# Attention scores as single float32 products, with deeper buffers and a new order table

## The chip, the cores and the metric

The kernel runs on one core of one Trainium2 chip. The metric is device time in microseconds (us) of one execution; lower is better. The engines are TensorE (PE in the profile; PEld are its weight loads), VectorE (DVE), ScalarE (ACT), GpSimd (POOL) and SyncE (SP), which here only issues DMAs.

## What is computed

Local and global attention for 4 batches, 8 heads, 512 local and 32 global tokens and a head size of 64, and behind it two networks over the 2,176 tokens of width 512:

```python
s_g = scale * q_g @ k_all.T;  out_g = softmax(s_g) @ v_all        # global rows see all 544 keys
s_ll = where(|i - j| <= 32, scale * q_l @ k_l.T, -1e9)            # local rows: a band,
out_l = softmax([scale * q_l @ k_g.T, s_ll]) @ [v_g, v_l]         # and the 32 global keys
x = concat(out_g, out_l)                                           # to (2176, 512)
x = (sigmoid(x @ w_gate) * (x @ w_val)) @ w_out                    # 1536 inner columns
h = x @ w_in;  out = (P(h) / (Q(h) + 1e-6)) @ w2_out               # 2048 inner columns; P, Q polynomials
```

The change touches the attention alone.

## The kernel before

**Stages.** `attention` comes first, then `gated` and `rational` (the two networks). TensorE takes its instructions in program order, so the networks' first matmul (line 539) stands behind the attention's last.

**Units.** The attention works on 16 units, one for a batch and a pair of heads. The 512 queries of a unit are 4 blocks of 128, each against a window of 224 keys. `units[u]` with even `u` also does the global rows of the units `u` and `u+1` (all steps whose name begins with `g_`).

**Split products.** A product of float32 precision is made as three products of `F32R` parts: high by high, high by low, low by high (`three`, and the loop in `s_mm`). So `k_hi` and `q_hi` (ScalarE casts) and `k_lo` and `q_lo` (GpSimd differences) split what was loaded ahead of `s_mm`; `g_q` splits the global queries; `v_hi`, `v_lo`, `t_hi`, `t_lo` split the values and the transposed probabilities.

**Steps of a unit.** `s_mm` (scores of two blocks: a "half", each block as two heads on the two halves of the rows), `s_max` (adds the mask, takes the maxima, writes `p`), `s_exp`, `s_add` and `s_rec` (sums and reciprocals), `s_norm` (VectorE takes 3 of the half's 4 rows of `p`, GpSimd one), `t_mm` (transposes of `p` and of the global probabilities `pgn`), `t_hi`, `t_lo`, `v_mm` (times the values, 6 matmuls a block), `v_xs` and `v_xg` (local and global results out of PSUM), `x_out` (GpSimd splits both into `xh`, `xl`, the networks' input). `v_dma` moves the values of neighbour blocks.

**Order.** `STEPS` is a table of places in unit steps: step `name` of unit `u` stands at `u + place`, and all are written to the engines in the order of these places. `w_raw` to `w_lo` are the steps that fetch and split the networks' first four weights (`Weights`, unchanged), in the same table. Each engine takes its own instructions in this order.

**Places.** PSUM has four places of `[128, 2, 512]` (`pair`), handed round in the order in which steps ask for them: scores, global scores, transposes and results all take one, and a place comes free when VectorE or ScalarE has read it. In SBUF, most tiles have two buffers.

Of the kernel before, what the change touches and what calls it, by code (L numbers as in the profile page):

```python
# [35 lines left out]
def tile_of(tok):  # L36
# [13 lines left out]
    (-0.696, 'k_hi'),  # L50
    (-0.612, 'q_hi'),
    (-0.595, 'w_mag'),
    (-0.434, 'k_lo'),
    (-0.361, 'q_lo'),
    (-0.351, 'w_bits'),
    (-0.222, 'w_add'),
# [2 lines left out]
    (0.380, 's_max', 0),
    (0.465, 's_max', 1),  # L60
    (0.577, 's_exp', 0, (2, 3)),
    (0.725, 'load', 'v'),
    (0.746, 's_exp', 0, (0, 1)),
    (0.792, 's_add', 0),
    (0.836, 'g_mm'),
    (0.860, 's_exp', 1, (2, 3)),
    (0.878, 'g_max'),
    (0.912, 'v_hi'),
    (0.920, 's_rec', 0),
    (0.945, 'w_hi'),  # L70
    (0.962, 'v_lo'),
    (1.014, 'g_exp'),
    (1.053, 's_norm', 0, 0, 3),
    (1.061, 'g_add'),
    (1.165, 'g_rec'),
    (1.200, 's_exp', 1, (0, 1)),
    (1.224, 'w_lo'),
    (1.231, 'g_norm'),
    (1.276, 's_norm', 0, 3, 4),
    (1.333, 's_add', 1),  # L80
    (1.606, 't_mm', 0),
    (1.635, 's_rec', 1),
    (1.657, 't_hi', 0),
    (1.681, 't_lo', 0),
    (1.683, 't_mm', 1),
    (1.758, 's_norm', 1, 3, 4),
    (1.775, 'v_dma'),
    (1.845, 's_norm', 1, 0, 3),
    (1.859, 't_hi', 1),
    (1.862, 'v_mm', 0),  # L90
    (1.863, 't_mm', 2),
    (1.883, 't_lo', 1),
    (1.916, 'v_mm', 1),
    (1.990, 't_mm', 3),
    (2.026, 't_hi', 2),
    (2.032, 'v_xs', 0),
    (2.081, 'v_xg', 0),
    (2.113, 't_lo', 2),
    (2.117, 't_hi', 3),
    (2.199, 't_lo', 3),  # L100
    (2.593, 'v_mm', 2),
# [30 lines left out]

def attention(ctx, tc, ident, xh, xl, ins, other={}, others=0):
# [24 lines left out]

# [25 lines left out]
    def g_load(u, x):  # L184
        nc.sync.dma_start(dict(q=qgn, v=vgn)[x], ins[f"{x}_g"])

    def g_q(u):
# [1 line left out]
        t = st[u]["qg"] = [two.tile([128, 6 * SG], F32R, tag=f"qg{s}", name=f"qg{s}{u}") for s in "hl"]
        src = qgn[:, b, pr // 2]  # L190
        nc.scalar.mul(t[0], src, -0.125)
        nc.vector.scalar_tensor_tensor(t[1], src, -0.125, t[0].bitcast(F32), ALU.mult, ALU.subtract)
# [4 lines left out]

    def k_hi(u):
        k = st[u]["k"] = two.tile([128, 2, NBLK, WIN], F32R, tag="k", name=f"k{u}")
        nc.scalar.copy(k[:, 0], st[u]["kn"])  # L200

    def k_lo(u):
        k = st[u]["k"]
        nc.gpsimd.tensor_tensor(k[:, 1], st[u]["kn"], k[:, 0].bitcast(F32), ALU.subtract)

    def q_hi(u):
        s = st[u]
        s["qh"] = two.tile([128, NBLK, 128], F32R, tag="qh", name=f"qh{u}")
        nc.scalar.copy(s["qh"], s["qn"])

    def q_lo(u):
        s = st[u]
        s["ql"] = two.tile([128, NBLK, 128], F32R, tag="ql", name=f"ql{u}")
        nc.gpsimd.tensor_tensor(s["ql"], s["qn"], s["qh"].bitcast(F32), ALU.subtract)
# [152 lines left out]
    def v_xg(u, half):
        s = st[u]
        at = 0 if u % 2 else 256
        if half == 0:  # L370
# [4 lines left out]
        nc.vector.tensor_tensor(s["xg"], s["po"][:, 1, at : at + 64], s["xg"], ALU.add)

    def x_out(u):
        b, pr = units[u]
        xs, xg = st[u]["xs"].rearrange("p c t -> p (c t)"), st[u]["xg"]
        parts = [(slice(64 * j, 64 * j + 64), B * S + b * SG, xg[64 * j : 64 * j + 64, SG * j : SG * j + SG])  # L380
                 for j in range(2)]
        for t0, n in TILES:
            lo, hi = max(t0, b * S), min(t0 + n, (b + 1) * S)
            if lo < hi:
                parts.append((slice(0, 128), lo, xs[:, lo - b * S : hi - b * S]))
        for rows, tok, src in parts:
            i, off = tile_of(tok)
            n = src.shape[1]
            h, l = xh[i][rows, pr, off : off + n], xl[i][rows, pr, off : off + n]
            copy(h, src, rows)  # L390
            nc.gpsimd.tensor_tensor(l, src, h.bitcast(F32), ALU.subtract)
# [3 lines left out]
    steps = dict(g_q=g_q, load=load, k_hi=k_hi, k_lo=k_lo, q_hi=q_hi,  # L395
                 q_lo=q_lo, v_hi=v_hi, v_lo=v_lo, v_dma=v_dma, s_mm=s_mm, s_max=s_max, s_exp=s_exp, s_add=s_add,
                 s_rec=s_rec, s_norm=s_norm, g_mm=g_mm, g_max=g_max, g_exp=g_exp, g_add=g_add, g_rec=g_rec,
                 g_norm=g_norm, t_mm=t_mm, t_hi=t_hi, t_lo=t_lo, v_mm=v_mm, v_xs=v_xs, v_xg=v_xg, x_out=x_out)
# [1 line left out]
    for x in "qv":  # L400
        g_load(0, x)
    for u in range(2):
        load(u, "k")
        load(u, "q")
        other["w_raw"](u)
    for u in range(2):
        load(u, "v")
# [464 lines left out]
```

## Time and profile before

| | us |
|---|---|
| median of 3 runs (lowest, highest) | 1041.23 (1040.93, 1043.89) |
| the profiled execution | 1040.94 |
| its span in the trace | 1039.1 |
| attention, up to the networks' first matmul | 231.0 |
| networks, from there to the end of the span | 808.1 |

TensorE is busy for 94% of the span, VectorE 72%, ScalarE 62% and GpSimd 59%. These are means over two stages that differ, so the stages are to be read one by one.

### The profile page before, as it was taken

Reading aid. Unit: us, or ns where it says so; the run is one execution under the profiler, and the core shown is the slowest. Engines: PE = TensorE matmul, PEld = TensorE weight load, DVE = VectorE, ACT = ScalarE, POOL = GpSimd, SP = SyncE. Lnnn points to the kernel's source line nnn. Section 1 sums busy time; section 2 is a strip of 40 time slices with the busy share of each in tenths; the row PEclk is TensorE's granted clock in tenths of the full one; section 3 lists DMA queues with packets and bytes.
Section 4 is the critical chain, followed back from the end, with each engine's and each line's share of the span. In section 5 each row is a group of like instructions: output and inputs, shape, how many; then the busy total and the mean of one; then the engine's idle time right before and its main releaser. Section 6 shows DMA issues by size and latency. Waiting matters only on the chain.

```text
span 1039.1 us, 15083 instructions
## 1 busy us (share of the span) xinstructions
PE 975.2 (94%) x5184; PEld 866.9 (83%) x5184; DVE 745.9 (72%) x1364; ACT 646.2 (62%) x1312; POOL 611.5 (59%) x592
## 2 busy tenths in 40 slices
PE   4788878879999999999999999999999999999996
PEld 3667777768998988989989989889888988988895
DVE  5877777754766676666666743797778888888885
ACT  5788877754444444444444433887777777777783
POOL 6899999963444444443444443664457556665663
PEclk9999998999999999999999999999999999999999
DMA  7343334222443444344434441100220130010111
GB/s 258 102 110 110 110 110 109 74 72 61 144 158 125 129 156 133 130 151 133 142 122 152 139 156 58 65 1 7 87 70 1 41 122 1 1 61 22 41 71 62
DMA packets 55921, 98.65 MB, mean 95 GB/s; under 512 B 5284, under 2 KB 29988, under 8 KB 55844
## 3 DMA queue, kind: packets, MB, share of 16 engines
q1 hardware_dynamic: 55844, 97.69, 29.5%
q8 instruction: 41, 0.67, 0.3%
q14 instruction: 36, 0.29, 0.1%
HBM read 69.62 MB, written 21.23 MB: 87 GB/s over the span
## 4 chain that ended last, share of the span: by engine, by line
PE 73%; DVE 1%; POOL 1%; issue 1%; ACT 1%; POOLq 0%; DVEq 0%
PE rp L733 6%; PE rp L732 6%; PE rp L731 6%; PE rp L541 6%; PE rp L539 6%; PE rp L540 6%; PE pg L539 4%; PE pg L540 4%; PE pg L541 4%; PE pv L540 4%; PE pv L539 4%; PE pv L541 4%; PE p L584 4%; PE p L583 4%; PE p L582 4%
## 5 line engine op out<-in xcount | busy, mean ns | idle before, releaser
L663 POOL TENSOR_TENSOR v<-v,u 128x384 f32<-128x384 f32 (+1 forms) x80 | 96.3, 1204 | 112.7 <-ACT v L659 112.2
L706 POOL TENSOR_TENSOR rgl<-t,rgh 128x384 fp32r<-128x384 f32 (+1 forms) x80 | 96.0, 1200 | 37.4 <-POOL v L663 30.6
L570 ACT CAST gh<-t 128x384 fp32r<-128x384 f32 (+1 forms) x60 | 33.4, 557 | 124.8 <-DVE t L567 124.8
L567 DVE TENSOR_TENSOR t<-pv,t 128x384 f32<-128x384 f32 (+1 forms) x60 | 36.6, 610 | 77.7 <-PE pv L541 73.8
L671 DVE TENSOR_TENSOR t<-rp,t 128x384 f32<-128x384 f32 (+1 forms) x80 | 48.6, 608 | 54.3 <-ACT t L667 53.5
L656 ACT ACTIVATE u<-rp 128x384 f32<-128x384 f32 (+1 forms) x80 | 42.6, 532 | 65.8 <-PE rp L541 65.6
L692 DVE SCALAR_TENSOR_TENSOR v<-v,u 128x384 f32<-128x384 f32 (+1 forms) x80 | 78.8, 985 | 0.0
L696 DVE SCALAR_TENSOR_TENSOR t<-t,co,v 128x384 f32<-128x384 f32 (+1 forms) x80 | 74.1, 926 | 2.8
L276 ACT ACTIVATE p<-p,mx 128x224 f32<-128x224 f32 x128 | 60.5, 476 | 18.2 <-DVE mx L269 18.1
L339 PE MATMUL pspt<-ident,p 128*112 128x128 f32 x256 | 54.3, 306 | 17.5 <-DVE ptl L348 13.7
L571 DVE TENSOR_TENSOR gl<-t,gh 128x384 fp32r<-128x384 f32 (+1 forms) x60 | 39.4, 657 | 37.4 <-ACT gh L570 37.4
L659 ACT ACTIVATE v<-u,co 128x384 f32<-128x384 f32 (+1 forms) x80 | 60.3, 754 | 2.6
L680 ACT ACTIVATE u<-v,co 128x384 f32<-128x384 f32 (+1 forms) x80 | 52.7, 659 | 9.9 <-POOL v L663 9.8
L594 DVE TENSOR_TENSOR gacc<-p,gacc 128x384 f32<-128x384 f32 (+1 forms) x100 | 54.8, 604 | 4.6 <-PE p L584 4.6
L667 ACT ACTIVATE t<-rp,co 128x384 f32<-128x384 f32 (+1 forms) x80 | 55.8, 697 | 0.0
L688 DVE SCALAR_TENSOR_TENSOR v<-v,u 128x384 f32<-128x384 f32 (+1 forms) x80 | 55.3, 692 | 0.0
L339 PEld LDWEIGHTS pspt<-ident,p 128*112 128x112 f32 x256 | 35.8, 150 | 22.3 <-DVE ptl L348 15.5
L675 DVE SCALAR_TENSOR_TENSOR t<-t,co,rp 128x384 f32<-128x384 f32 (+1 forms) x80 | 52.7, 659 | 0.0
L348 DVE TENSOR_TENSOR ptl<-pspt,pth 112x640 fp32r<-112x640 f32 x64 | 51.4, 814 | 1.0 <-ACT pth L344 0.5
L344 ACT CAST pth<-pspt 112x640 fp32r<-112x640 f32 x64 | 43.9, 686 | 12.9 <-PE pspt L340 10.6
L684 ACT ACTIVATE u<-u,co 128x384 f32<-128x384 f32 (+1 forms) x80 | 51.9, 648 | 0.0
L702 ACT CAST rgh<-t 128x384 fp32r<-128x384 f32 (+1 forms) x80 | 43.5, 544 | 5.6 <-DVE t L696 5.6
(594 smaller groups left out, 3594.4 us busy)
## 6 DMA issues: line engine op xcount, KB each, us to landing
raw2in<-in_w_in SPq DMA_DIRECT2D x16, 512.0 KB, 3.8
raw2out<-in_w_out SPq DMA_DIRECT2D x16, 512.0 KB, 3.6
kn<-in_k_l SPq DMA_DIRECT2D x16, 448.0 KB, 3.6
raw1gate<-in_w_gate SPq DMA_DIRECT2D x12, 512.0 KB, 4.0
raw1val<-in_w_val SPq DMA_DIRECT2D x12, 512.0 KB, 3.5
raw1out<-in_w_out SPq DMA_DIRECT2D x12, 512.0 KB, 3.6
out<-racc SPq DMA_DIRECT2D x17, 256.0 KB, 2.0
qn<-in_q_l SPq DMA_DIRECT2D x16, 256.0 KB, 2.9
```

The source lines that it names most:

```text
L276: nc.scalar.activation(p, p, AF.Exp, bias=s["mx", half][:, n : n + 1], scale=-1.0, accum_out=s["sm", half][:, n : n + 1])
L339: nc.tensor.transpose(ps[0:CH, k, at + j * 128 : at + (j + 1) * 128], s["p"][:, c, j, cols], ident)
L539: nc.tensor.matmul(ps, wh[:, w], mh[:, k], start=k == 0, stop=False)
L540: nc.tensor.matmul(ps, wh[:, w], ml[:, k], start=False, stop=False)
L541: nc.tensor.matmul(ps, wl[:, w], mh[:, k], start=False, stop=k == 3)
L663: nc.gpsimd.tensor_tensor(s["v"], s["v"], s["u"], ALU.mult)
L692: nc.vector.scalar_tensor_tensor(s["v"], s["v"], 2.0, s["u"], ALU.subtract, ALU.mult)
L696: nc.vector.scalar_tensor_tensor(s["t1"], s["t1"], a0, s["v"], ALU.add, ALU.mult)
L706: nc.gpsimd.tensor_tensor(s["gl"], s["t1"], s["gh"].bitcast(F32), ALU.subtract)
L731: nc.tensor.matmul(ps, gh[:, w], wh, start=k == 0, stop=False)
L732: nc.tensor.matmul(ps, gh[:, w], wl, start=False, stop=False)
L733: nc.tensor.matmul(ps, gl[:, w], wh, start=False, stop=k == G - 1)
```

## The change

- `k_hi`, `k_lo`, `q_hi`, `q_lo` and `g_q` go. `s_mm` and `g_mm` multiply `qn` and `kn` (`qgn` and `kn`), float32 as loaded, with one `matmul` where there were three. In the compiled program each such float32 `matmul` is two pairs of weight load and matmul, an `F32R` one is one pair: 5,184 pairs before, 5,024 now.
- The scale of the global scores, which `g_q` applied, moves to `g_exp` and to a new step `g_neg` on GpSimd between `g_max` and `g_exp`.
- `s_norm` gives 2 of the 4 rows to each engine.
- `p`, `pth` and `ptl` get a third buffer; `kn` has 4, `qn` 3. `v_mm` keeps its two halves under two names.
- The global results of a batch are gathered in `xga` by `v_xg` and split once a batch, not once a unit.
- `qgn` is loaded for two units at a time, the loads at the start come in another order, and all places in `STEPS` are new.

```diff
 STEPS = [
...
-    (-1.768, 'load', 'q'),
-    (-1.014, 'load', 'k'),
+    (-3.228, 'load', 'k'),
+    (-3.026, 'load', 'q'),
...
-    (0.040, 's_mm', 0),
-    (0.341, 's_mm', 1),
+    (-0.800, 's_mm', 0),
+    (-0.292, 's_mm', 1),
...
-    (2.623, 'v_mm', 3),
+    (1.885, 'v_mm', 3),
...
+KEPT = dict(k=4, q=3, v=2)
...
     def s_mm(u, half):
...
-            s["p"] = two.tile([128, NBLK, 2, WIN], F32, tag="p", name=f"p{u}")
+            s["p"] = two.tile([128, NBLK, 2, WIN], F32, tag="p", name=f"p{u}", bufs=3)
...
-            for n, (x, y) in enumerate((("qh", 0), ("qh", 1), ("ql", 0))):
-                for j in range(2):
-                    rows = slice(64 * j, 64 * j + 64)
-                    nc.tensor.matmul(ps[:, j, i * WIN : (i + 1) * WIN], s[x][rows, c],
-                                     s["k"][rows, y, c], start=n == 0, stop=n == 2)
+            for j in range(2):
+                rows = slice(64 * j, 64 * j + 64)
+                nc.tensor.matmul(ps[:, j, i * WIN : (i + 1) * WIN], s["qn"][rows, c], s["kn"][rows, c],
+                                 start=True, stop=True)
...
     def g_mm(u):
...
-                w = [t[:, 64 * i : 64 * i + 128] for t in st[u]["qg"]]
-                three(ps[:, at : at + n], *w, *(keys(st[u + i]["k"], y) for y in range(2)), i == 0, i == 1)
+                nc.tensor.matmul(ps[:, at : at + n], st[u]["qgn"][:, 64 * i : 64 * i + 128], keys(st[u + i]["kn"]),
+                                 start=i == 0, stop=i == 1)
...
+    def g_neg(u):
+        t = st[u]["gmx"]
+        nc.gpsimd.tensor_scalar_mul(t, t, -0.125)
...
+            for j in range(2):
+                rows, cols = slice(64 * j, 64 * j + 64), slice(j * SG, (j + 1) * SG)
+                nc.vector.tensor_tensor(xga[b % 2][rows, pr], ps[rows, 1, at : at + 64][:, cols], s["xg"][rows, cols],
+                                        ALU.add)
...
+    def split(tok, prs, src):
+
+        i, off = tile_of(tok)
+        h, l = (t[i][:, prs, off : off + src.shape[-1]] for t in (xh, xl))
+        copy(h, src)
+        nc.gpsimd.tensor_tensor(l, src, h.bitcast(F32), ALU.subtract)
...
     def x_out(u):
...
+        if pr == NPAIR - 1:
+            split(B * S + b * SG, slice(0, NPAIR), xga[b % 2])
```

GpSimd, one unit in the middle of the attention, before (`k` and `ql` are the low parts of keys and queries, `p` the probabilities, `xg` the global results, `r` and `gr` sums to be inverted):

```order
L223 TENSOR_TENSOR v_915<-vn_865,v_915 128x512
L315 TENSOR_SCALAR gr_966<-gsm_942 128x1
L325 TENSOR_TENSOR pgn_94<-pg_943,gr_966 128x4x128
L327 TENSOR_TENSOR pgn_94<-pg_943,gr_966 128x32
L290 TENSOR_TENSOR p_766<-p_766,r_0_877 128x224
L281 TENSOR_SCALAR r_1_984<-sm_1_801 128x4
L204 TENSOR_TENSOR k_982<-kn_931,k_982 128x896
L214 TENSOR_TENSOR ql_1041<-qn_792,qh_1005 128x512
L290 TENSOR_TENSOR p_766<-p_766,r_1_984 128x224
L281 TENSOR_SCALAR r_0_1068<-sm_0_952 128x4
L167 TENSOR_TENSOR xh_72<-xg_968,zero 64x32
L391 TENSOR_TENSOR xl_77<-xg_968,xh_72 64x32
```

And now, from one `g_neg` (line 283) to the next `x_out`:

```order
L283 TENSOR_SCALAR gmx_1270<-gmx_1270 128x1
L255 TENSOR_SCALAR r_0_1313<-sm_0_1185 128x4
L293 TENSOR_SCALAR gr_1331<-gsm_1315 128x1
L264 TENSOR_TENSOR p_1039<-p_1039,r_1_1285 128x448
L264 TENSOR_TENSOR p_1182<-p_1182,r_0_1313 128x448
L303 TENSOR_TENSOR pgn_92<-pg_1316,gr_1331 128x4x128
L305 TENSOR_TENSOR pgn_92<-pg_1316,gr_1331 128x32
L198 TENSOR_TENSOR v_1348<-vn_1194,v_1348 128x512
L166 TENSOR_TENSOR xh_68<-xs_1262,zero 128x512
L370 TENSOR_TENSOR xl_73<-xs_1262,xh_68 128x512
```

The 896 and 512 wide differences of lines 204 and 214 and the four 64x32 pieces are gone; both `s_norm` pieces are 448 wide and stand side by side.

TensorE between the transposes of one unit and the scores of a later one, before (`pspt` transposes, `pss` scores, `pspv` results):

```order
L339 MATMUL pspt_3_386<-ident,p_150 112x128 x2
L340 MATMUL pspt_3_386<-ident,pgn_94 112x128
L260 MATMUL pss_0_398<-k_272,qh_295 128x224 x4
L260 MATMUL pss_0_398<-k_272,ql_322 128x224 x2
L260 MATMUL pss_0_398<-k_272,qh_295 128x224 x4
L260 MATMUL pss_0_398<-k_272,ql_322 128x224 x2
L260 MATMUL pss_1_430<-k_272,qh_295 128x224 x4
L260 MATMUL pss_1_430<-k_272,ql_322 128x224 x2
L260 MATMUL pss_1_430<-k_272,qh_295 128x224 x4
L260 MATMUL pss_1_430<-k_272,ql_322 128x224 x2
```

And now, from the last two matmuls of a `v_mm` on (`psgl` are global scores):

```order
L219 MATMUL pspv_0_291<-ptl_1_247,vb_90 128x320
L220 MATMUL pspv_0_291<-pth_1_246,vb_90 128x320
L272 MATMUL psgl_321<-kn_127,qgn_131 128x512
L272 MATMUL psgl_321<-kn_161,qgn_131 128x512
L272 MATMUL psgl_321<-kn_127,qgn_131 128x32
L272 MATMUL psgl_321<-kn_161,qgn_131 128x32
L234 MATMUL pss_1_334<-kn_127,qn_129 128x224 x4
L218 MATMUL pspv_2_364<-pth_2_280,v_191 128x320
L219 MATMUL pspv_2_364<-ptl_2_281,v_191 128x320
```

The scores of a unit's two halves no longer stand together: the second half (`pss_1`) comes behind the global scores, and a score takes one row for 4 float32 matmuls where it took two rows of `F32R` ones twice.

SP's first DMAs before (`raw1gate` and `raw1val` are weights, `vn` values):

```order
L788 DMA ident<-in_ident 128x128
L148 DMA masks<-in_masks 128x672
L185 DMA qgn<-in_q_g 128x1536
L185 DMA vgn<-in_v_g 128x512
L177 DMA kn_109<-in_k_l 128x896
L177 DMA qn_111<-in_q_l 128x512
L464 DMA raw1gate_113<-in_w_gate 128x4x256
L177 DMA kn_115<-in_k_l 128x896
L177 DMA qn_117<-in_q_l 128x512
L464 DMA raw1val_119<-in_w_val 128x4x256
L177 DMA vn_121<-in_v_l 128x512
L177 DMA vn_123<-in_v_l 128x512
```

And now, up to the first global queries:

```order
L176 DMA kn_106<-in_k_l 128x896
L176 DMA qn_108<-in_q_l 128x512
L389 DMA masks<-in_masks 128x672
L390 DMA ident<-in_ident 128x128
L452 DMA raw1gate_112<-in_w_gate 128x4x256
L176 DMA vn_114<-in_v_l 128x512
L393 DMA vgn<-in_v_g 128x512
L176 DMA kn_117<-in_k_l 128x896
L176 DMA qn_119<-in_q_l 128x512
L452 DMA raw1val_121<-in_w_val 128x4x256
L185 DMA qgn_125<-in_q_g 128x192
```

The keys and queries of unit 0 moved to the front; the global queries, which were third, are now eleventh, behind the first two weights.

## Rows read from the trace of the kernel before

**Rows 1.** the page of the profile, its head.

```profile
span 1039.1 us, 15083 instructions
```

**Rows 2.** busy time by stages: length, engine busy (instructions), granted clock, DMA.

```profile
core 0: us, PE busy (x) PEld busy (x) DVE busy (x) ACT busy (x) POOL busy (x), PEclk, DMA share, GB/s
...
33.00:201.00 168.00, 141.70 (x1037) 124.86 (x1037) 128.21 (x390) 135.36 (x375) 153.94 (x197) 0.93 0.39 107
...
231.00:1039.10 808.10, 798.32 (x3936) 713.07 (x3936) 580.75 (x876) 473.89 (x842) 415.29 (x334) 1.00 0.27 88
```

**Rows 3.** timeline of TensorE: start us, busy us, instruction, idle before.

```profile
39.24 0.39 PE L260 MATMUL pss<-k,qh 64*128 64x224 f32 x4
...
39.58 0.38 PE L260 MATMUL pss<-k,qh 64*128 64x224 f32 x4
...
41.33 0.38 PE L339 MATMUL pspt<-ident,p 128*112 128x128 f32 x2
...
41.66 0.38 PE L339 MATMUL pspt<-ident,p 128*112 128x128 f32 x2
...
42.58 0.31 PE L244 MATMUL pspv<-ptl,vb 112*128 112x320 f32 x1
...
42.72 0.31 PE L245 MATMUL pspv<-pth,vb 112*128 112x320 f32 x1
...
43.45 0.48 PE L243 MATMUL psgl<-k,qgh 128*128 128x512 f32 x1
...
45.41 0.26 PE L245 MATMUL psgl<-k,qgl 128*128 128x32 f32 x1
...
229.29 0.31 PE L245 MATMUL pspv<-pth,vb 112*128 112x320 f32 x1
...
231.01 0.50 PE L539 MATMUL pg<-xh,w10gate 128*128 128x512 f32 x1 [1.41 <-ACT xs L365]
```

**Rows 4.** GpSimd's groups, 33 to 201 us: count | busy us, mean ns | idle before.

```profile
L204 POOL TENSOR_TENSOR k<-kn,k 128x896 fp32r<-128x896 f32 x13 | 27.5, 2114 | 1.6 <-ACT k L200 0.6
L214 POOL TENSOR_TENSOR ql<-qn,qh 128x512 fp32r<-128x512 f32 x13 | 21.9, 1683 | 0.0
L290 POOL TENSOR_TENSOR p<-p,r 128x224 f32<-128x224 f32 x26 | 18.2, 701 | 0.0
...
L391 POOL TENSOR_TENSOR xl<-xg,xh 64x32 fp32r<-64x32 f32 x25 | 13.6, 544 | 2.0
...
L325 POOL TENSOR_TENSOR pgn<-pg,gr 128x512 f32<-128x512 f32 x6 | 6.2, 1039 | 1.4 <-DVE gr L319 1.4
L167 POOL TENSOR_TENSOR xh<-xg,zero 64x32 fp32r<-64x32 f32 x25 | 5.9, 234 | 1.7
```

**Rows 5.** who waited for whom, 33 to 201 us: total us, times, longest.

```profile
DVE gr L319 <- POOL gr L315: 14.3, 6, 3.1
...
PE pspt L339 <- DVE ptl L348: 11.1, 5, 2.6
```

**Rows 6.** ScalarE's groups, 33 to 201 us.

```profile
L200 ACT CAST k<-kn 128x896 fp32r<-128x896 f32 x13 | 12.1, 930 | 0.0
L209 ACT CAST qh<-qn 128x512 fp32r<-128x512 f32 x13 | 8.0, 616 | 0.0
...
L191 ACT ACTIVATE qgh<-qgn 128x192 fp32r<-128x192 f32 x5 | 1.8, 361 | 0.0
```

**Rows 7.** VectorE's groups, 33 to 201 us.

```profile
L290 DVE TENSOR_TENSOR p<-p,r 128x672 f32<-128x672 f32 x28 | 29.9, 1068 | 0.5
...
L192 DVE SCALAR_TENSOR_TENSOR qgl<-qgn,qgh 128x192 fp32r<-128x192 f32 x5 | 6.0, 1207 | 0.0
```

**Rows 8.** line 290: duration in ns, min/median/max.

```profile
L290 DVE TENSOR_TENSOR p<-p,r x32: 843/858/1836, 22.3 to 220.0; 128x672 f32<-128x672 f32 x32
```

**Rows 9.** timeline of ScalarE at the start.

```profile
8.26 0.94 ACT L200 CAST k<-kn 128x896 fp32r<-128x896 f32 x1 [0.22 <-DMA kn<-in_k_l]
...
10.64 0.66 ACT L475 ACTIVATE v1gate<-raw1gate 128x512 f32<-128x512 f32 x1 [0.87 <-DMA raw1gate<-in_w_gate]
```

More of the change, by code (lines that the diff above doesn't have):

```diff
@@ L45 @@
 STEPS = [
-    (-2.490, 'g_q'),
-    (-1.956, 'w_raw'),
-    (-1.768, 'load', 'q'),
-    (-1.014, 'load', 'k'),
[L50 to L56, printed above, removed]
-    (0.040, 's_mm', 0),
-    (0.341, 's_mm', 1),
[L59 to L101, printed above, removed]
-    (2.623, 'v_mm', 3),
-    (2.655, 'v_xg', 1),
-    (2.749, 'v_xs', 1),
@@ L105 @@
-    (2.942, 'x_out'),
+    (-3.228, 'load', 'k'),
+    (-3.026, 'load', 'q'),
+    (-2.954, 'g_load'),
+    (-0.800, 's_mm', 0),
+    (-0.657, 'load', 'v'),
+    (-0.470, 's_max', 0),
+    (-0.386, 'g_mm'),
+    (-0.363, 'w_raw'),
+    (-0.292, 's_mm', 1),
+    (-0.230, 'g_max'),
+    (-0.230, 's_exp', 0, (2, 3)),
+    (-0.202, 's_max', 1),
+    (-0.100, 's_exp', 0, (0, 1)),
+    (-0.067, 'g_neg'),
+    (-0.048, 's_add', 0),
+    (-0.046, 'g_exp'),
+    (0.191, 'g_add'),
+    (0.218, 's_rec', 0),
@@ new lines @@
+    (0.227, 'g_rec'),
+    (0.357, 'v_hi'),
+    (0.402, 's_exp', 1, (0, 1)),
+    (0.462, 's_norm', 0, 2, 4),
+    (0.531, 's_norm', 0, 0, 2),
+    (0.544, 'g_norm'),
+    (0.565, 's_exp', 1, (2, 3)),
+    (0.654, 'v_lo'),
+    (0.785, 'v_dma'),
+    (0.844, 's_add', 1),
+    (0.858, 't_mm', 0),
+    (0.909, 's_rec', 1),
+    (1.058, 't_mm', 1),
+    (1.091, 't_hi', 0),
+    (1.174, 's_norm', 1, 0, 2),
+    (1.248, 't_hi', 1),
+    (1.307, 'w_mag'),
+    (1.387, 's_norm', 1, 2, 4),
+    (1.425, 't_lo', 0),
@@ L106 @@
+    (1.451, 't_lo', 1),
+    (1.457, 't_mm', 2),
+    (1.468, 't_hi', 2),
+    (1.481, 'v_mm', 0),
+    (1.517, 't_mm', 3),
+    (1.579, 't_hi', 3),
+    (1.584, 'v_mm', 1),
+    (1.625, 'w_bits'),
+    (1.640, 't_lo', 2),
+    (1.659, 't_lo', 3),
+    (1.714, 'v_xs', 0),
+    (1.740, 'v_xg', 0),
+    (1.855, 'v_mm', 2),
+    (1.885, 'v_mm', 3),
+    (2.205, 'v_xs', 1),
+    (2.364, 'v_xg', 1),
+    (2.422, 'w_add'),
+    (2.690, 'w_hi'),
+    (2.753, 'x_out'),
+    (2.930, 'w_lo'),
 ]
@@ L147, in attention @@
     masks = one.tile([128, 3, WIN], F32, name="masks")
-    nc.sync.dma_start(masks, ins["masks"])
     mask_of = [masks[:, 0]] + [masks[:, 1]] * (NBLK - 2) + [masks[:, 2]]
@@ L175, in load, with g_load @@
             shape = [128, NBLK, WIN] if x == "k" else [128, NBLK, 128]
-            t = st[u][f"{x}n"] = two.tile(shape, F32, tag=f"{x}n", name=f"{x}n{u}")
+            t = st[u][f"{x}n"] = two.tile(shape, F32, tag=f"{x}n", name=f"{x}n{u}", bufs=KEPT[x])
             nc.sync.dma_start(t, ins[f"{x}_l"][b, pr])
-    qgn = one.tile([128, B, NPAIR // 2, 6 * SG], F32, name="qgn")
     vgn = two.tile([128, H * D], F32, tag="xs", name="vgn")
     vg = one.tile([128, 2, H * D], F32R, name="vg")
-    def g_load(u, x):
-        nc.sync.dma_start(dict(q=qgn, v=vgn)[x], ins[f"{x}_g"])
-    def g_q(u):
+    def g_load(u):
         b, pr = units[u]
[L189 to L192, printed above, removed]
+        st[u]["qgn"] = two.tile([128, 6 * SG], F32, tag="qgn", name=f"qgn{u}")
+        nc.sync.dma_start(st[u]["qgn"], ins["q_g"][b, pr // 2])
     def g_v(u):
@@ L196, in g_v @@
         nc.gpsimd.tensor_tensor(vg[:, 1], vgn, vg[:, 0].bitcast(F32), ALU.subtract)
[L198 to L214, printed above, removed]
     def v_hi(u):
@@ L330, in t_mm @@
         s = st[u]
-        s["th", c] = two.tile([CH, 2, 320], F32R, tag="pth", name=f"pth{u}_{c}")
-        s["tl", c] = two.tile([CH, 2, 320], F32R, tag="ptl", name=f"ptl{u}_{c}")
+        s["th", c] = two.tile([CH, 2, 320], F32R, tag="pth", name=f"pth{u}_{c}", bufs=3)
+        s["tl", c] = two.tile([CH, 2, 320], F32R, tag="ptl", name=f"ptl{u}_{c}", bufs=3)
         ps = pair(f"pspt{u}_{c}")
@@ L352, in v_mm @@
         if c % 2 == 0:
-            s["po"] = pair(f"pspv{u}_{c}")
+            s["po", c // 2] = pair(f"pspv{u}_{c}")
+        po = s["po", c // 2]
         for k in range(2):
             w = [(s["v"][0:CH], s["vb"])[k][:, i, c] for i in range(2)]
-            three(s["po"][:, c % 2, 0:320], *w, s["th", c][:, k], s["tl", c][:, k], first=k == 0, last=k == 1)
+            three(po[:, c % 2, 0:320], *w, s["th", c][:, k], s["tl", c][:, k], first=k == 0, last=k == 1)
     def v_xs(u, half):
@@ L384, in x_out @@
             if lo < hi:
[L385 to L391, printed above, removed]
+                split(lo, pr, xs[:, lo - b * S : hi - b * S])
+        if pr == NPAIR - 1:
+            split(B * S + b * SG, slice(0, NPAIR), xga[b % 2])
         st[u].clear()
     n = len(units)
[L395 to L398, printed above, removed]
+    steps = dict(g_load=g_load, load=load, v_hi=v_hi, v_lo=v_lo, v_dma=v_dma, s_mm=s_mm, s_max=s_max, s_exp=s_exp,
+                 s_add=s_add, s_rec=s_rec, s_norm=s_norm, g_mm=g_mm, g_max=g_max, g_neg=g_neg, g_exp=g_exp, g_add=g_add,
+                 g_rec=g_rec, g_norm=g_norm, t_mm=t_mm, t_hi=t_hi, t_lo=t_lo, v_mm=v_mm, v_xs=v_xs, v_xg=v_xg, x_out=x_out)
     steps.update(other)
[L400 to L407, printed above, removed]
+    load(0, "kq")
+    nc.sync.dma_start(masks, ins["masks"])
+    nc.sync.dma_start(ident, ins["ident"])
+    other["w_raw"](0)
+    load(0, "v")
+    nc.sync.dma_start(vgn, ins["v_g"])
+    load(1, "kq")
+    other["w_raw"](1)
     g_v(0)
```

25 lines of the change are left out of this document (13 added, 12 removed).

## The prediction

> **What bounds the kernel now.** I read the head of the page first: the span is 1039.1 us [rows 1], 1.84 us less than the profiled execution (1040.94), which is 0.29 below the median of the runs (1041.23). The sums below start from 1040.94. The busy times by stages come next [rows 2]. From 231 us on TensorE is busy for 798.3 of 808.1 us at the full clock. The change leaves the networks alone, so these 808 us stay, and what the change does is the shift of the networks' first matmul, which stands at 231.0 [rows 3].
>
> In the attention's middle, 33 to 201 us, GpSimd is the fullest engine: 153.9 of 168 us, 92%; ScalarE has 81%, VectorE 76%, TensorE 84% by records that overlap [rows 2]. The pace comes from TensorE's timeline: the last `v_mm` matmul of unit 0 starts at 42.72, that of unit 15 at 229.29, so a unit takes 186.57 / 15 = 12.44 us [rows 3]. GpSimd's busy time in it is 0.92 x 12.44 = 11.4 us, and the others wait for its queue: VectorE stood 14.3 us in 6 waits for the one-column sum `gr`, which takes GpSimd a fraction of a microsecond but is queued behind its wide differences [rows 5]. So GpSimd sets the pace here. Behind it stands a second ring: `t_mm` waits for places and operands that `t_lo` on VectorE gives (11.1 us) [rows 5].
>
> **What the change does to each engine, per unit of 12.44 us.**
>
> *GpSimd.* It loses `k_lo` (2.11 us), `q_lo` (1.68) and the global pieces, two of 0.54 and two of 0.23 (1.56) [rows 4]: 5.35. It gains in `s_norm`: two pieces of 448 columns for two of 224 at 0.70; a 512-wide product of the same kind takes 1.04 [rows 4], so 448 take some 0.92 undisturbed, 1.14 if they are slowed as the 0.70 is now; I take 1.14, which adds 0.88. The global split of a batch is two pieces of 128 columns; at most two of 1.04 in four units, 0.5, and I take 0.4. `g_neg`, once in two units, is of the size of the smallest pieces (0.23): 0.12. Sum 11.4 - 5.35 + 1.4 = 7.45. GpSimd is no longer the bound.
>
> *ScalarE.* It loses `k_hi` 0.93, `q_hi` 0.62 and half a `g_q`, 0.18 [rows 6]: 1.73 of 0.81 x 12.44 = 10.0, which leaves 8.3.
>
> *VectorE.* It loses half a `g_q`, 0.6, and a third of each `s_norm` [rows 7]. The 672 columns take 843 ns undisturbed, 1836 at worst and 1068 on average [rows 7, 8], so 448 take 0.56 to 0.71 us; by the dearer 0.36 is saved twice. `v_xg` has one small instruction more, 0.2. Of 0.76 x 12.44 = 9.5 us, 8.4 are left. That the long ones stand beside GpSimd's long differences is what the spread from 843 to 1836 suggests. The Trainium skill, page "GPSIMD Engine Reference", says that GpSimd shares its SBUF interfaces with VectorE, with contention in instructions that read two SBUF inputs. These rows agree; a shorter list of VectorE from a less busy GpSimd is left out of the sum.
>
> *TensorE.* By the distance of starts at full clock [rows 3]: the scores take 0.34 us for six matmuls, 1.36 for a unit's 24; transposes 0.33 for three, 2.64 for 24; `v_mm` 0.145 each, 3.5 for 24; a `g_mm` from 43.45 to 45.41 and one short step, 2.07, half of it a unit, 1.03. Sum 8.55. The mean granted clock of the stage is 0.93 of full speed [rows 2], between its levels of 1.2 and 2.4 GHz, so the list takes about 8.55 / 0.93 = 9.2 us. Two 224-column score matmuls start in 0.113 us where one of 320 columns takes 0.145: the two heads of a pair run beside each other. No row shows a float32 product other than a transpose. From below: a compiled float32 product is two pairs of load and matmul, and at the pace of today's pairs the scores would take two thirds of 1.36. From above: two instructions that each stream twice as long and lose the running side by side would take 2.7 times 1.36, 3.6 us. The nearest row is the three-part product that computes the same thing; I take its price, so that TensorE keeps its 9.2 us, and keep both ends. The Trainium skill, page "FP8 and Floating Point Precision", section "TensorE Precision Notes", gives true float32 four passes through the array where the split product has three; by it scores and global scores would cost a third more. That speaks against the change, and is a rival below.
>
> *Loads and places.* The third `p`, `pth` and `ptl`, and four `kn` and three `qn`, cost no instruction. The loads are the same bytes but for `qgn`; at a shorter pace the DMA share rises from 0.39 [rows 2] to 0.45. SP's loads of `k` stand 3.2 unit steps ahead and wait for the fourth-last user, some 34 us of cover; without it a unit would begin with a load that takes several microseconds.
>
> *A wait that is added.* `g_neg` stands on GpSimd behind an `x_out` of two wide pieces, 2.4 us at most, and ScalarE's `g_exp`, with the next `t_hi` queued behind it, waits for it. Bound: 0 to 1.2 us a unit. `x_out` has its input half a unit earlier by the table and GpSimd has 3 us of slack, so I take 0.
>
> **The pace after.** TensorE 9.2, VectorE 8.4, ScalarE 8.3, GpSimd 7.45, and the first three are tied through four PSUM places and the `t_hi`, `t_lo`, `v_mm` chain. GpSimd, outside that ring, reached 92%; ScalarE, inside, 81% without being the bound. I choose 85% for the fullest engine: 9.2 / 0.85 = 10.8 us. Over 15 units that is 15 x (12.44 - 10.8) = 24.6 us.
>
> **The start.** The first `k` landed at 8.26, the first weight, 768 KB later in the queue, at 10.64 [rows 9]: 323 KB a microsecond, with 2,648 KB through by then. Unit 0's scores now start when its `k` and `q`, the first 704 KB, are in, but its second half stands behind `g_mm`, which needs the eleventh load: 3,448 KB, (3448 - 2648) / 323 = 2.5 us after 10.64, at 13.1. `g_mm` at half clock takes 4.1 us: 17.2. From there the table has about 2.2 unit steps to the last `v_mm` of unit 0; with the light load of the beginning I count 8.4 us (VectorE's list) for each: 18.5, so 35.7 for 42.72 now. That is 7 us gained, between 0 (the load order eats it) and 10. The end of the attention keeps its 1.7 us from the last `v_mm` to 231.0 [rows 3].
>
> Sum: 1040.94 - 24.6 - 7.0 = 1009.3.
>
> **Rivals.**
> - *The engines mesh as well as GpSimd alone did.* 92% of 9.2 gives 10.0 us: -36.6 - 7 gives 997. For it: third buffers and halves apart. Against it: the ring's waits [rows 5].
> - *Float32 takes four thirds of today's TensorE time, still in pairs side by side*: 0.45 + 0.35 us a unit, 9.35 / 0.93 = 10.05, at 85% 11.8: -9.6 - 7 gives 1024. The rule of the Trainium skill's page on floating point, above, would have it so.
> - *The ring keeps the old pace.* Then only the start is gained: 1034. For it: PSUM still has four places and `t_mm` waited for `t_lo`; against it: GpSimd at 92% explains the pace alone.
> - *Float32 takes four passes and no longer runs two heads side by side.* 32 passes of 0.113 are 3.6 us for the scores, 0.35 more for the global ones: 8.55 + 2.26 + 0.35 = 11.2, / 0.93 = 12.0, and TensorE alone at 92% needs 13.0: +8.4 - 7 gives 1042, no change that can be measured. For it: no row shows float32 in pairs; against it: the rows of the array are addressed as before.
> - *Slower: the clock.* If TensorE is granted less in this stage, its list stretches: 8.55 / clock / 0.92 must reach 12.44 + 7 / 15 = 12.9 before the gain is gone, which is a mean clock of 0.72. At 0.70 the time is 1046, at the lower level throughout (0.50) 18.6 us a unit and 1126. For it: the stage already has 0.93; against it: TensorE will be fuller, not emptier.
>
> **Chances.** Forecast 0.50, meshing 0.12, four thirds side by side 0.18, old pace 0.05, four passes one by one 0.08, clock 0.07. A change of 0.3% (3.1 us) is about what a measurement of this kernel can tell. The first four are faster: 0.85; the fifth is the same: 0.08; the last slower: 0.07. The range from 994 to 1034 holds the forecast, the two that end at 1024 and 1034, and the better part of the meshing case; the two dear cases at the top are left out.
>
> **What would show it.** The granted clock of the stage at 0.93 or above; the networks' first matmul near 199 us; the last `v_mm` of units 0 and 15 some 162 us apart; GpSimd's share in the middle near 70%, with TensorE the fullest at about 85%; the wait of `gr` for GpSimd gone from the top; float32 score matmuls of a half whose starts span about 0.7 us. Wrong if a half's scores span 1.5 us or more, if the networks' stage is not 808 us, or if waits of `g_exp` for `g_neg`, or of TensorE for PSUM places, take what GpSimd gives back.

## The result and the profile after

The changed kernel takes 1001.48 us (median of four runs, 1001.22 to 1002.30); the kernel before took 1041.08 beside it. The ratio is 0.9615, 95% interval 0.9598 to 0.9633: 39.6 us less. The head of the page of after, which answers to [rows 1]:

```profile
span 999.0 us, 14595 instructions
...
PE 963.5 (96%) x5024; PEld 850.9 (85%) x5024; DVE 728.1 (73%) x1372; ACT 622.5 (62%) x1272; POOL 550.8 (55%) x512
```

Busy time by stages of the kernel after (columns as in [rows 2]):

```profile
core 0: us, PE busy (x) PEld busy (x) DVE busy (x) ACT busy (x) POOL busy (x), PEclk, DMA share, GB/s
33.00:80.00 47.00, 38.38 (x239) 33.20 (x236) 38.14 (x115) 33.98 (x94) 35.96 (x39) 0.85 0.50 145
80.00:165.00 85.00, 84.79 (x590) 70.62 (x589) 73.67 (x261) 77.30 (x232) 68.66 (x93) 1.00 0.48 132
33.00:165.00 132.00, 123.17 (x827) 103.83 (x824) 111.81 (x375) 111.28 (x324) 104.62 (x132) 0.95 0.49 136
```

GpSimd, the fullest engine before, has 104.62 of 132 us, 79%, where it had 92% [rows 2]. The stretch falls in two. From 80 us on TensorE is busy throughout by its records, at full clock; up to 80 us it has 82% at a granted clock of 0.85. TensorE's timeline of after, at the places of [rows 3]:

```profile
12.99 4.08 PE L272 MATMUL psgl<-kn,qgn 128*128 128x512 f32 x8 [6.34 <-DMA qgn<-in_q_g]
17.00 2.54 PE L234 MATMUL pss<-kn,qn 64*128 64x224 f32 x24
...
35.51 0.31 PE L220 MATMUL pspv<-pth,vb 112*128 112x320 f32 x1
...
102.66 2.25 PE L272 MATMUL psgl<-kn,qgn 128*128 128x512 f32 x8
...
104.83 1.03 PE L234 MATMUL pss<-kn,qn 64*128 64x224 f32 x8
105.79 0.41 PE L218 MATMUL pspv<-pth,v 112*128 112x320 f32 x1
...
189.05 0.31 PE L220 MATMUL pspv<-pth,vb 112*128 112x320 f32 x1
190.97 0.47 PE L527 MATMUL pg<-xh,w10gate 128*128 128x512 f32 x1 [1.61 <-DVE xga L362]
```

The rows of scores count eight instructions for four products in a half, and 24 in the first, whose neighbours merge with it. A half's scores start 0.96 us ahead of what follows them (104.83 to 105.79), the global scores 2.17 ahead (102.66 to 104.83). The last `v_mm` of unit 0 stands at 35.51 and that of unit 15 at 189.05, so a unit takes 153.54 / 15 = 10.24 us on average, where it took 12.44. The units are not alike: from one unit's last `v_mm` to the next one's it is 14.1, 14.7, 13.2 and 10.9 us up to 88 us, and then 8.7 to 8.9 and 10.7 in turn, up to the last two (7.4 and 6.7). Those in turn are called the dense units below. The networks begin at 190.97, 40.0 us earlier than before, and take 808.0 us as they did.

GpSimd and VectorE normalize now in pieces of 448 columns; the groups of after, 33 to 165 us, first GpSimd's, then VectorE's (answering to [rows 4] and [rows 7]):

```profile
L264 POOL TENSOR_TENSOR p<-p,r 128x448 f32<-128x448 f32 x24 | 26.6, 1123 | 6.0 <-DVE r L259 5.7
```

```profile
L264 DVE TENSOR_TENSOR p<-p,r 128x448 f32<-128x448 f32 x24 | 17.4, 724 | 0.4
```

And who waited for whom in after, 33 to 165 us (columns as in [rows 5]), from the top of the list:

```profile
DVE xg L359 <- ACT xs L345: 14.3, 12, 2.5
ACT pth L322 <- PE pspt L318: 11.4, 10, 3.4
PEld pspv L218 <- DVE ptl L326: 10.5, 17, 3.8
POOL gmx L283 <- DVE gmx L279: 9.4, 6, 4.2
PE pspv L218 <- DVE ptl L326: 6.7, 3, 3.4
...
ACT pg L289 <- POOL gmx L283: 4.2, 7, 1.8
```

The wait of `gr` for GpSimd has left the top. The longest one now, VectorE's `xg` behind ScalarE's `xs`, was there before with 14.2 us in 12 waits; from 80 us on it stands beside a TensorE that is busy throughout.

### The profile page after: what moved, and what is told of

It is laid out like the page before. It is cut to its first block, busy times and chain, and to the rows that moved or that the text cites. A ratio compares the mean times of both kernels' runs of the same rounds, so it can differ in the third digit from the quotient of the medians.

```text
span 999.0 us, 14595 instructions
## 1 busy us (share of the span) xinstructions
PE 963.5 (96%) x5024; PEld 850.9 (85%) x5024; DVE 728.1 (73%) x1372; ACT 622.5 (62%) x1272; POOL 550.8 (55%) x512
## 4 chain that ended last, share of the span: by engine, by line
PE 76%; DVE 1%; POOL 1%; issue 1%; ACT 1%; DVEq 0%; POOLq 0%
PE rp L721 6%; PE rp L720 6%; PE rp L719 6%; PE rp L529 6%; PE rp L527 6%; PE rp L528 6%; PE pg L527 5%; PE pg L529 5%; PE pg L528 5%; PE pv L529 5%; PE pv L527 5%; PE pv L528 5%; PE p L572 4%; PE p L571 4%; PE p L570 4%
## 5 line engine op out<-in xcount | busy, mean ns | idle before, releaser
L322 ACT CAST pth<-pspt 112x640 fp32r<-112x640 f32 x64 | 43.8, 687 | 16.2 <-PE pspt L318 15.8
L317 PE MATMUL pspt<-ident,p 128*112 128x128 f32 x256 | 48.3, 285 | 2.6 <-ACT p L250 2.6
L243 DVE CUSTOM_DVE_ANT_0 p<-pss,masks 128x224 f32<-128x224 f32 x128 | 42.1, 384 | 7.0 <-PE pss L234 7.0
```

## The experiments

Every time is a median beside runs of the kernel before on the same chip, which took 1041.1 to 1041.5; the ratio is to those. Two theories stood against each other. *Relief*: the float32 products take work from GpSimd, and the rest is free. *Places and order*: the third places and the new table let the engines mesh, and the products matter less. A waiting time below is from the profiled execution.

**Two places (e1_buf2).** The kernel after, with the third places taken back:

```diff
-            s["p"] = two.tile([128, NBLK, 2, WIN], F32, tag="p", name=f"p{u}", bufs=3)
+            s["p"] = two.tile([128, NBLK, 2, WIN], F32, tag="p", name=f"p{u}")
...
```

The same goes for `pth` and `ptl`.

> The changed kernel with two places instead of three for p, pth and ptl. Relief theory (the pace was GpSimd's splitting work, and TensorE bounds now): the places are used only when TensorE would otherwise stand, a loss of 2 to 8 us, 1003 to 1010. Rival, order theory (table and buffers brought the gain): half of the 40 us go, 1015 to 1025.

Measured: 1020.45 us, ratio 0.9800 [0.9785, 0.9815], 19.0 above after. The list of waits of this kernel, 33 to 165 us, has a new row:

```profile
ACT pth L322 <- PE pspt L318: 16.8, 12, 5.1
...
DVE p L243 <- PE pspt L317: 11.0, 9, 1.6
...
PE pspv L218 <- DVE ptl L326: 9.8, 5, 4.5
...
PE psgl L272 <- DVE mx L243: 2.7, 5, 0.5
PE pss L234 <- DVE mx L243: 2.7, 5, 0.5
```

VectorE's `s_max`, which writes `p`, waits for the transposes that still read the place's last `p`. TensorE stands in turn, for VectorE's maxima (new in the list) and for `t_lo` (6.7 us in 3 waits in after). From 80 us on it is busy 79.38 us of 85, at 0.97:

```profile
80.00:165.00 85.00, 79.38 (x532) 65.91 (x532) 65.35 (x231) 66.61 (x194) 61.61 (x79) 0.97 0.45 125
```

The time lies in the range of the order theory.

**A third place for p alone (e9_p3).** The same edit on `pth` and `ptl` only.

> The changed kernel with a third place for p alone; pth and ptl have two places again. With two places for all three the time was 1020.4, 19 above the change, and the new wait on the list was s_max's write of p behind the transposes that read the place's last p (11.0 us in 9 waits), with nothing new in front of t_hi and t_lo for their places. If p's place is what the order needs, p alone gives the 19 us back: 1001 to 1006, and that wait is gone. If the order needs the places of pth and ptl as well, it stays between: 1010 to 1020, with ScalarE's t_hi or VectorE's t_lo waiting for TensorE's v_mm.

Measured: 1005.74 us, ratio 0.9658 [0.9644, 0.9673]. So `p` brings 14.7 of the 19.0 us and the other two 4.3. That lies at the upper edge of the first case. The wait for `p` is gone from the list; what the 4.3 us wait for was not taken apart.

**Split products in the new order (e2_split).** Two places, and the split products back with their casts and differences 0.7 to 1.0 unit steps ahead of the scores. By the sizes in the two kernels the split parts take 25 KB of a partition and the third places 12 KB; no run here has both in SBUF. `kn` and `qn` have one place fewer here, so the products are not the only difference to the kernel of e1.

```diff
...
+    (-1.800, 'g_q'), (-1.750, 'k_hi'), (-1.700, 'q_hi'), (-1.600, 'k_lo'), (-1.500, 'q_lo'),
...
-KEPT = dict(k=4, q=3, v=2)
+KEPT = dict(k=3, q=2, v=2)
...
```

> The kernel of the run with two places, and in it the products of split parts again, with their casts and differences 0.7 to 1.0 unit steps ahead of the scores. Relief theory: GpSimd has 3.8 us a unit more, 7.8 + 3.8 = 11.6, at 92% a pace of 12.6, so 33 us or more over the run with two places, 1035 to 1045. Order theory: TensorE's list is shorter by 0.6 us a unit and the rest is hidden, within 10 us of the run with two places.

Measured: 1052.41 us, ratio 1.0110 [1.0095, 1.0126], 32.0 above the kernel with two places and float32 products, and above the kernel before. Its stages:

```profile
33.00:80.00 47.00, 35.49 (x235) 30.99 (x235) 37.10 (x99) 34.32 (x93) 37.73 (x38) 0.83 0.50 141
80.00:165.00 85.00, 65.28 (x493) 57.65 (x492) 61.72 (x193) 65.16 (x181) 71.80 (x75) 0.92 0.38 106
```

From 80 us on TensorE has 65.28 of 85 us, and GpSimd is the fullest with 84%. The difference is close to that of the relief theory (33 or more); the time lies above the ranges of both. Of the 32.0 us some 10 are in the start: unit 0's last `v_mm` stands at 47.16, in e1 at 37.43. A unit takes 12.77 us, in e1 11.26.

**The float32 products alone (e4_float_alone).** The kernel before, its table and its two places, with the scores as in after; `k_hi`, `k_lo`, `q_hi`, `q_lo` and `g_q` go, `g_neg` stands ahead of `v_hi`.

> The kernel before with the float32 products alone (no casts and differences of q and k, g_neg added; table, places, s_norm, global results and loads as before). Relief theory: GpSimd falls to 7.7 us a unit and the pace to that of a full TensorE with an order made for other lists, 10.5 to 11.5: 1041 - 15 to 29, 1012 to 1026. Order theory: 1035 or more.

Measured: 1022.09 us, ratio 0.9812 [0.9796, 0.9829]: 19.0 us gained in the old order.

Its stage from 80 us on:

```profile
80.00:165.00 85.00, 76.41 (x512) 63.53 (x511) 62.19 (x210) 63.65 (x191) 63.43 (x101) 0.96 0.42 122
```

GpSimd has 75% here and TensorE, the fullest, 90%. Unit 0's last `v_mm` stands at 36.94, so 5.8 of the 19.0 us come in the start, with the old order of loads. Along this path the 39.6 us divide into 19.0 for the products, 1.6 for all other edits with two places (table, loads, `s_norm`, `xga`), and 19.0 for the third places. The 1.6 are not clear of noise, since the intervals of e4 and e1 overlap. The shares hold for this path: third places with split products, or in the old table, were not tried. The two theories are not rivals in the end: each is right about some half of the gain.

**Each product twice (e3_double).** The output is the same; TensorE's part of the scores doubles.

```diff
+                for _ in range(2):
...
                     nc.tensor.matmul(ps[:, j, i * WIN : (i + 1) * WIN], s["qn"][rows, c], s["kn"][rows, c],
```

> The changed kernel with each score product made twice (same result): 1.92 us a unit more on TensorE and nothing on any other engine. If TensorE bounds the whole pace now: +1.92 x 15 = 29 us, 1030. If it bounds only from 80 us on, as the windows suggest (8 or 9 of 16 units): +16 to +22, 1018 to 1023. If VectorE or GpSimd still holds the pace: under +8.

Measured: 1017.19 us, ratio 0.9772 [0.9758, 0.9787], 15.7 above after, just under the second case. A half's scores take 1.82 us where after has 0.96, so 1.7 us a unit were added, not the 1.92 expected. The dense units take 12.2 and 10.1 us in turn where after has 10.7 and 8.7: some 1.45 of the added 1.7 us arrive in the pace, so TensorE sets it from 80 us on. The units ahead of 80 us (12.8, 14.3, 12.2, 12.2) did not become longer on the whole (14.1, 14.7, 13.2, 10.9 in after): something else sets them. Unit 0's last `v_mm` comes 5.2 us later.

**Head by head (e5_apart).** Of a half's four products, head 0's two are written ahead of head 1's two, where after alternates.

```diff
...
-        for i in range(2):
-            c = 2 * half + i
-            for j in range(2):
-                rows = slice(64 * j, 64 * j + 64)
+        for j in range(2):
+            rows = slice(64 * j, 64 * j + 64)
+            for i in range(2):
+                c = 2 * half + i
...
```

> The changed kernel with the scores of a half ordered head by head (both blocks of one head, then both of the other), so that neighbours on TensorE use the same rows of the array. If two float32 products on the two halves of the rows run beside each other: a half's eight matmuls, which start within 0.96 us now, take 1.4 us or more, +0.8 us a unit, +7 to +13 us, 1008 to 1014. If they run one after another anyway: no change, within 2 us.

Measured: 1002.47 us, ratio 0.9625 [0.9610, 0.9639], no change, and the dense units are the same. I read this at first as: the heads do not run side by side. The next experiment put that reading aside.

**Both heads from the same rows (e11_rows).** The scores of the second head are left out; the first head's stand in both places.

```diff
-                rows = slice(64 * j, 64 * j + 64)
+                rows = slice(0, 64)
```

> The changed kernel with both heads' local score products taken from head 0's rows (the second head's scores are left out; same number and size of instructions, to the same places). A half's eight float32 instructions of 224 columns take 0.96 us, and their records start in pairs 0.19 us apart. If an instruction takes 0.09 us by itself, one after another, nothing changes: 1000 to 1004, a half 0.96. If each takes 0.19 us and the two heads run side by side in their halves of the rows, a half takes 0.75 us more, 1.5 a unit, as much as doubling the products added: 1014 to 1022, a half 1.6 to 1.8.

Measured: 1018.36 us, ratio 0.9788 [0.9757, 0.9819], 16.9 above after. Two rows of TensorE's timeline:

```profile
110.33 1.78 PE L234 MATMUL pss<-kn,qn 64*128 64x224 f32 x8
112.03 0.41 PE L218 MATMUL pspv<-pth,v 112*128 112x320 f32 x1
```

A half takes 1.70 us where after has 0.96. The instruction records themselves start, in us from a half's first:

```
after      0  0.007  0.293  0.300  0.483  0.489  0.672  0.678
e5_apart   0  0.013  0.293  0.306  0.482  0.495  0.671  0.685
e11_rows   0  0.293  0.483  0.672  0.861  1.050  1.239  1.428
```

So one float32 instruction of 224 columns takes 0.19 us, and two heads do run side by side, each in its half of the rows. They do so even where the program has all of head 0 ahead of head 1. Whether the compiled program or TensorE brings them together there is not shown.

**Two undone parts.** The global results split per unit, not once a batch (e8_globunit):

> The changed kernel with the global results split once a unit again (two 32-column pieces a unit instead of two 128-column pieces in four units): 0.5 us a unit more on GpSimd. Relief theory with TensorE as bound: under 2 us. If GpSimd's queue still holds the pace: 5 us or more.

Measured: 1003.34 us (997.36 to 1004.07), ratio 0.9619 [0.9591, 0.9648]: not to be told from after. The loads of the start in the order of first use (e7_start; `g_load(0)` and unit 1's `k` ahead of `v`, and all of these and unit 1's `q` ahead of `ident` and the two weights):

> The changed kernel with the first global queries and unit 1's keys loaded ahead of the weights. If the wait of 6.3 us for the eleventh load sets the start: g_mm starts at 8 us instead of 13, 3 to 5 us gained, 997. If VectorE, ScalarE or the weights set the filling: within 1.5 us.

Measured: 996.17 us (992.66 to 997.99), ratio 0.9559 [0.9537, 0.9581], 5.3 below after. In after the first global products wait 6.34 us for `qgn` in the row at 12.99 above, and that load stood behind both weights; here they start at 7.58. The profiled execution, the slowest of the four, has the networks 2.9 us earlier than after.

**The weights' steps (e6_spread, e10_best, e12_best2).** In after's slow units TensorE stands behind this part of VectorE's queue, with TensorE's row behind it:

```profile
41.10 1.26 DVE L471 TENSOR_SCALAR v1val<-v1val 128x512 f32<-128x512 f32 x1
42.40 1.37 DVE L472 TENSOR_SCALAR v1val<-v1val 128x512 uint32<-128x512 uint32 x1
43.80 0.69 DVE L473 SCALAR_TENSOR_TENSOR v1val<-raw1val,v1val 128x512 uint32<-128x512 uint32 x1
44.41 0.82 DVE L326 TENSOR_TENSOR ptl<-pspt,pth 112x640 fp32r<-112x640 f32 x1
```

```profile
40.82 1.03 PE L234 MATMUL pss<-kn,qn 64*128 64x224 f32 x8
45.28 0.63 PE L218 MATMUL pspv<-pth,v 112*128 112x320 f32 x1 [3.43 <-DVE ptl L326]
```

The three steps of a weight (3.3 us) stand ahead of `t_lo`, and `v_mm` waits 3.43 us for it. First, one weight in three units and not one in each (`3 * u + place` for the weights' steps):

> The changed kernel with the early weights' steps spread, one weight in three units instead of one in each. If the weights' VectorE work in front of t_lo is what makes the first units slow (12 us a unit between 33 and 80 us against 9.7 behind) and the fall of the granted clock follows from it: 8 to 14 us gained, 988 to 994. If the start is slow for another reason (loads, filling): within 3 us.

Measured: 1000.79 us (999.42 to 1002.61), ratio 0.9605 [0.9586, 0.9623]. That is the case of no gain, but not for its reason. The first units fall to 8.8 and 11.1 us, and later ones rise to 13.8 and 12.7. From unit 0 to unit 10 it is 110.8 us where after has 111.4: the blocks cost as much wherever they stand. So the block was taken apart, with e7's loads, a weight in every second unit:

```diff
...
-    (1.625, 'w_bits'),
+    (1.362, 'w_bits', 0), (2.362, 'w_bits', 1), (3.362, 'w_bits', 2),
...
```

`w_add`, `w_hi` and `w_lo` follow the last of them.

> The changed kernel with the loads of the start in the order of first use (that alone gave 996.2) and each weight's three VectorE steps (1.26, 1.37 and 0.69 us) taken apart: one in each of three units, just ahead of the second half's v_xg, where VectorE stood idle 1.2 to 2.5 us behind ScalarE's xs, and a new weight every second unit. If the first 45 us after unit 0 are slow because the three steps stand as a block ahead of t_lo (units of 13 to 15 us against 8.7 to 10.7 later), the units up to 80 us fall to 10 to 11 us and the time to 982 to 990. If the block only stands there and the early units are slow by the granted clock or the loads, the time stays within 2 us of 996.2. If a step in a gap delays v_xg, and with it the PSUM place that the next scores wait for, it is 997 to 1003.

Measured: 993.44 us, ratio 0.9538 [0.9524, 0.9552], in none of the three ranges. It is 2.7 below e7, not clear of noise, since the intervals overlap. In the profiles unit 0's last `v_mm` comes 3.8 us earlier than in e7, and the ten units behind it take 109.6 us for 111.2. The networks take 1.6 us longer in this profile; the granted clock is 0.50 from 182.7 to 186.1 us here, which by itself costs 1.7 us, and 1.00 at that place in e7. Every second unit up to 97 us still takes 12.9 to 14.5 us. VectorE's and TensorE's rows of this kernel in one of them:

```profile
63.49 0.43 DVE L479 TENSOR_SCALAR v1gate<-v1gate 128x512 f32<-128x512 f32 x1 [1.64 <-ACT v1gate L470]
63.83 0.69 DVE L483 SCALAR_TENSOR_TENSOR v1val<-raw1val,v1val 128x512 uint32<-128x512 uint32 x1
64.44 0.22 DVE L364 TENSOR_TENSOR xg<-pspv,xg 128x64 f32<-128x64 f32 x1
64.69 0.39 DVE L367 TENSOR_TENSOR xga<-pspv,xg 64x32 f32<-64x32 f32 x2
```

```profile
65.22 0.40 PE L322 MATMUL pspt<-ident,p 128*112 128x128 f32 x2 [2.21 <-DVE xga L367]
```

ScalarE's steps of the next weight had begun at 62.80, and VectorE stood for them. With `w_mag` at 0.700 in place of 1.307:

> The kernel with the early loads and the weights' VectorE steps taken apart (993.4), with one move more: ScalarE's two steps of each weight 0.6 units earlier. In that kernel every second unit up to 97 us took 12.9 to 14.5 us against 8.8 for the ones between, and in one of the long ones VectorE stood 1.6 us at the weight's first step for ScalarE's, which had begun just ahead of it, and TensorE then 2.2 us for VectorE's xga. If that wait makes the long units long, three of them lose some 2 us each: 985 to 989. If the long units are long because ScalarE has two steps of 0.7 us more in them wherever these stand, the time stays at 992 to 995.

Measured: 988.71 us (988.20 to 991.01), ratio 0.9492 [0.9477, 0.9506], the fastest here, 4.7 below e10. The ten units behind unit 0 take 105.7 us. The stages of this kernel:

```profile
33.00:80.00 47.00, 42.48 (x298) 35.22 (x297) 43.58 (x137) 41.72 (x121) 38.41 (x45) 1.00 0.52 150
80.00:165.00 85.00, 81.45 (x572) 68.40 (x573) 75.03 (x260) 75.34 (x224) 69.86 (x95) 1.00 0.44 119
```

Up to 80 us TensorE has 42.48 us for 38.38, and the granted clock 1.00 for 0.85.

## Why the prediction was right, and which term was mis-sized

The forecast was 1009.3, and 1001.5 came, inside the range and on the forecast side. By its steps:

- *The start* came as summed: unit 0's last `v_mm` at 35.51 for 35.7, `g_mm` at 12.99 for 13.1 and 4.08 us long for 4.1, the scores behind it at 17.00 for 17.2. The gain is 7.2 us for 7.0. It is not the gain of the new loads, though: e4 has 5.8 us of it with the old ones, and e2, with the new loads and split products, is 4.4 us later than before. So most of it is the products'.
- *GpSimd is no longer the bound*: right, and shown by both sides (19.0 us in the old order, 32.0 in the new). Its share is 79% where 70% was named, and that is not only the shorter pace: 79% of 10.24 is 8.1 us a unit, where the list had 7.45. The 448-wide piece takes 1.12 us for 1.14, VectorE's 0.72 for 0.71; pieces of `x_out` took longer than before (1.46 us for 1.35 at 512 columns), and the rest was not taken apart.
- *The pace* is the mis-sized term: 10.24 us a unit for 10.8, 33.0 us gained for 24.6. Two parts of it missed, in opposite directions.
- *The price of a float32 product* was set at that of three split parts, 1.36 us of scores a unit; two halves of 0.96 make 1.92. The two are not measured alike: 1.36 is by the distance of starts, 0.96 runs to the start of what follows. Before, the scores of a unit took 1.53 us in that measure, where nothing held up their second half:

```profile
38.81 0.48 PE L260 MATMUL pss<-k,qh 64*128 64x224 f32 x4
...
40.34 0.41 PE L243 MATMUL pspv<-pth,v 112*128 112x320 f32 x1
```

So the products cost 0.39 us a unit more, a quarter, and the rest of the 0.56 was missing in the list. The rival with four thirds had this part (it added 0.45 us to the scores), and it named the right mechanism, pairs side by side (e11). From 0.19 us for 224 columns at the granted 1.00, the level of 2.4 GHz, I estimate that an instruction streams its columns twice (2 x 224 / 2.4 = 187 ns), and a product has two. The global products agree: the starts of those with 512 columns lie 0.43 us apart after and 0.23 before. That is the four passes of the Trainium skill, page "FP8 and Floating Point Precision", section "TensorE Precision Notes": the rows here agree. The global product rose only from 2.07 to 2.17 us. Four long instructions of 0.43 us took the place of six of 0.23, and four of 32 columns that of six, at 0.11 us each in both kernels.

- *The fill of 85%* was the larger miss. With the dearer products the list is 8.55 + 0.56 + 0.05 = 9.16 us (the terms of the 8.55 add to 8.53 as written); at the measured clock of 0.95, 9.64; of the pace of 10.24 that is 94%. The step that failed is the choice between 92% for an engine outside the ring and 81% for one inside it: I said that the third places cost no instruction and gave them no gain, but they are what loosens the ring (e1, e9: 19.0 us, `p` most of all). With two places the same list fills 87% of a unit's 11.26 us, at the clock of 0.94 that e1 has from 33 to 165 us. With the true list and 85% the sum would have been 9.16 / 0.93 / 0.85 = 11.6 us and 1021, the time that two places give. So the forecast owes its nearness in part to luck: a price too low and a fill too low offset each other. With the fill alone put right, 8.55 / 0.93 / 0.94 = 9.8 us a unit, it would have been 994. The meshing rival (997) had the fill right.
- *No wait took its place*: `g_exp` for `g_neg` is in the list as `pg` for `gmx`, 4.2 us in seven waits, inside its bounds. The networks' 808 us stayed. The clock rival did not come: the mean rose from 0.93 to 0.95.
- *What the prediction did not see*: up to 80 us the weights' steps, which the change moved in the table, hold `t_lo` and TensorE up. With their VectorE steps taken apart, their ScalarE steps earlier and the loads of the start in order (e12), 12.8 us are gained; 5.3 of them are the loads (e7), and the 7.5 are not divided further, because e10 is not clear of e7.

The granted clock of 0.85 up to 80 us has not been taken apart from the waits: with them gone it is 1.00 (e12), and with more work for TensorE in the same order 0.94 (e3). In after it is 0.50 in three stretches there, 13.7 us in all, from 43.8, 60.9 and 74.5 us; the first of them:

```profile
43.81:50.64 6.83, 5.36 (x22) 5.25 (x23) 4.54 (x16) 2.53 (x9) 4.83 (x6) 0.50 0.73 214
```

TensorE had stood for 3.4, 2.1 and 3.1 us, from 41.9, 57.4 and 70.7 us on. In e12 its longest stand from 33 to 165 us is 1.6 us, and no such stretch follows. That the stands bring the lower clock is not shown by itself.

## What to carry to other kernels

An edit that removes tiles can pay twice, once by the work and once by places for other tiles; here each was worth 19.0 us along the path tried. Look which wait is for a place, and price it as one. When the bound moves to another engine, its fill is a term to bound from both sides: here the miss in it was worth 1.1 us a unit (9.64 / 0.85 against 10.24), the dearer products 0.6. A block of small steps in a queue costs by what stands behind it; here dividing it into gaps gained clearly only when the steps' own operands were ready there.

## What was not expected of the hardware

Two float32 products from different halves of the rows run side by side (a pair of instructions each 0.19 us) even where the program writes all of one half first (starts 0.013 us apart in e5_apart, 0.19 apart in e11_rows from one half alone). With TensorE's scores doubled (e3) the granted clock of the stretch from 33 to 80 us was 0.94 and not 0.85, and these units were no longer than before.

The prediction read the long normalizations of VectorE as standing beside GpSimd's long differences. The records say more exactly what happens: the one that comes second waits for the first. All of line 264 in after, ns:

```profile
L264 DVE TENSOR_TENSOR p<-p,r x32: 619/626/1302, 20.7 to 182.4; 128x448 f32<-128x448 f32 x32
```

```profile
L264 POOL TENSOR_TENSOR p<-p,r x32: 929/934/1368, 19.6 to 182.4; 128x448 f32<-128x448 f32 x32
```

The 13 of VectorE's that took 665 to 1302 ns each began while a tensor-by-tensor instruction of GpSimd was under way, and ended 0.48 us after that one did. The other 19 took 619 to 626 ns. GpSimd's took 929 to 935 ns unless one of VectorE's had begun just ahead, and then 1228 to 1368. So GpSimd's piece of `s_norm` pays when it stands beside VectorE's (15 of 32), and VectorE's pays when a difference or a copy of GpSimd is ahead of it (13 of 32). The means of 724 and 1123 ns are mixtures of such cases.
